# A spectral mixing and feed-forward kernel: batch 0's inverse stage in float32, decode steps, small loads and buffers moved

## The chip, the cores and the metric

The kernel runs on one core of a Trainium2 chip. The metric is the time of one execution in device microseconds (us); lower is better.

## What is computed

```python
def _attn_ref(x, w_r, w_i, b_r, b_i):
    X = np.fft.rfft(x, axis=1)
    Xr, Xi = (X.real.astype(np.float32), X.imag.astype(np.float32))
    Yr = Xr @ w_r - Xi @ w_i + b_r
    Yi = Xr @ w_i + Xi @ w_r + b_i
    lam = 0.01
    Yr = np.sign(Yr) * np.maximum(np.abs(Yr) - lam, 0.0)
    Yi = np.sign(Yi) * np.maximum(np.abs(Yi) - lam, 0.0)
    Y = Yr.astype(np.float64) + 1j * Yi.astype(np.float64)
    y = np.fft.irfft(Y, n=x.shape[1], axis=1)
...
def _moe_ref(x, mu_k, mu_r, w_k, w_v, w_r):
...
    xk = mu_k * x + (1.0 - mu_k) * x_prev
    xr = mu_r * x + (1.0 - mu_r) * x_prev
    k = np.maximum(xk @ w_k, 0.0)
    v = k * k @ w_v
    r = 1.0 / (1.0 + np.exp(-(xr @ w_r)))
    return (r * v).astype(np.float32)
...
def _moe2_ref(x, w_in, w_out):
    h = x @ w_in
    relu6 = np.clip(h + 3.0, 0.0, 6.0)
    g = h * relu6 / 6.0
    return (g @ w_out).astype(np.float32)
```


A Fourier mix along 3072 places, then two feed-forward blocks, for 4 batches of 256 columns. The weights of the second and third part arrive as 64-bit floats. The result has to be close to float32, so most products are made from a high and a low float32r part of each side: three matmuls (high by high, low by high, high by low) for one.

## The kernel before

**Stages.** The transform of 3072 = 96 x 32 places is done as matmuls with tables. For each batch: *s1* (`s1`, 8 steps; a step is two float32 matmuls of 96 rows by 512 columns) goes from x to the scratch `sc_a` in DRAM; *mid* (12 steps) reads `sc_a` and writes `sc_b`; *ib* (8 steps) reads `sc_b` and writes `sc_y`. A middle step j has three parts: `s2` (four float32 matmuls with a table tile `tt`, then `split` into Xh by ScalarE and Xl by VectorE), `mix` (24 float32r matmuls with the weights aw; then yf on VectorE, ym on ScalarE and again yf on VectorE, which is bias and shrinkage; then a split into yh and yl) and `ia` (12 float32r matmuls with the inverse half of a later table tile, an evacuation by ScalarE into iasb, a store). In the loop of `mid` step j issues s2(j), mix(j-1) and ia(j-2).

Behind that come the feed-forward blocks: *units* of a tile of 512 places, `u_r` (pr, one block of twelve 512-column matmuls), four times `u_k` (pk) and `u_v` (acc), into `sc_x`; then the third part (pi, rq, cc, oacc) to the output. A `u_k` makes g = relu, gh = g squared rounded to float32r, g = g squared, gl = g - gh.

**Order.** PE, ScalarE (ACT), VectorE (DVE) and POOL run what the program writes, in the order in which it is written; `stream(first)` is batch 0 up to its first two ib steps, `stream(later)` the rest, one step per unit. So batch 0 runs nearly alone (the *fill*), the others between the units of the batch before them. While batch 0 runs, the weights of the second part are loaded (`stw`) and decoded from the bits of 64-bit floats: `decode` is a generator whose parts (four on VectorE, two on ScalarE, then a split) are advanced by `next(loads)` in the steps listed in `DECODE`. The weights of the third part are decoded the same way (`jobs2`) between the last units, once the stream has ended.

**Queues and buffers.** SyncE (SP) issues nearly all loads and stores, POOL the tables `tt`, f1, fi and tex. A load or store also waits until the one that used its completion counter before it (there are eight, taken in turn) has landed. `load_chunks` keeps `AHEAD` loads of `a` in front of their use, in `AHEAD + 2` buffers. PSUM has two banks in pool `pa` (acc, oacc) and three slots of two banks in `ps`, which s1, s2, mix, ia, ib, pr and pk take in turn; a slot is free when its last reader is done. The tag `ev` gives three buffers for evacuations that are stored: s1sb, iasb, ysb. A tile is written again only when the store from it has landed.

In the trace both s1 and s2 have tiles named s: s1's are on L295, s2's on L332. mix and ia are on the helper's line L164.

## Time and profile before

| | |
|---|---|
| median of 3 runs | 2021.54 us (2019.42 to 2022.19) |
| profiled execution | 2019.82 us, of which 2018.1 are its span |
| busy: TensorE, VectorE, ScalarE, POOL | 98%, 70%, 61%, 2% of the span |
| granted clock of TensorE, mean | 0.99 |
| moved by DMA | 166.26 MB, mean 82 GB/s |

The span runs from the first to the last instruction. Busy time of TensorE is counted from the start of a matmul to its end, and neighbours overlap, so a busy TensorE may still be slow; the granted clock is a share of full speed, 0.50 being 1.2 GHz and 1.00 being 2.4 GHz. "Idle before <- X" names what ended the idle time of an engine. The chain of waits is followed back from the last instruction to what released each step.

### The profile page before, as it was taken

What the parts mean: (1) busy time and instruction counts of PE and PEld (TensorE: products, weight loads), DVE (VectorE), ACT (ScalarE), POOL (GpSimd) and SP (SyncE); (2) the same over time, 40 slices, a digit from 0 to 9 for tenths busy, and PEclk for the clock granted to TensorE, in tenths of its full rate; (3) what the DMA queues carried; (4) which work ended last, traced back from release to release, by engine and by line L of the source; (5) the groups of instructions that cost most, each with busy time, mean ns of one, the idle gap of its engine ahead of it and who ended that gap; (6) DMA issues with size and microseconds to landing.
All of it is one profiled execution on the core that took longest, in us unless ns stands there. A gap on an engine that the chain in (4) does not pass through costs nothing.

```text
span 2018.1 us, 33029 instructions
## 1 busy us (share of the span) xinstructions
PE 1970.9 (98%) x13656; PEld 1812.8 (90%) x13656; DVE 1417.5 (70%) x1721; ACT 1228.0 (61%) x1757; POOL 34.6 (2%) x63
## 2 busy tenths in 40 slices
PE   6789999999999999999999999999999999999998
PEld 4768987988798888777899999999999999999998
DVE  0756654565465658787878877788777887778776
ACT  2556555455445546666557766677667676676665
POOL 0000000000000000000000000000000000000000
PEclk8879999999999999999999999999999999999999
DMA  9675437444643342222101100011001010010100
GB/s 281 198 225 172 118 113 217 150 115 139 210 133 95 107 149 84 76 70 88 42 22 33 32 22 22 25 29 33 22 22 29 25 32 22 22 32 25 30 11 22
DMA packets 106712, 166.26 MB, mean 82 GB/s; under 512 B 12945, under 2 KB 62994, under 8 KB 106562
## 3 DMA queue, kind: packets, MB, share of 16 engines
q1 hardware_dynamic: 96034, 141.76, 22.6%
q0 software_dynamic: 10208, 22.13, 4.5%
q8 instruction: 107, 1.75, 0.4%
q14 instruction: 43, 0.35, 0.1%
q10 hardware_dynamic: 320, 0.26, 0.0%
HBM read 100.81 MB, written 63.31 MB: 81 GB/s over the span
## 4 chain that ended last, share of the span: by engine, by line
PE 81%; DVE 11%; ACT 5%; DMA 2%; issue 1%; ACTq 0%; SPq 0%; DVEq 0%; POOLq 0%
PE oacc L824 25%; PE rq L824 16%; PE acc L164 9%; PE pk L164 8%; PE cc L824 6%; PE mix L164 5%; PE ib L437 3%; PE s L332 3%; PE pr L164 2%; PE s L295 2%; DVE g L574 2%; DVE gl L575 2%; PE ia L164 1%; PE pi L164 1%; ACT gh L573 1%
## 5 line engine op out<-in xcount | busy, mean ns | idle before, releaser
L824 PE MATMUL oacc<-wo_hi,gl 128*128 128x256 f32 x1536 | 425.6, 277 | 1.2 <-DVE gl L765 1.2
L824 PE MATMUL oacc<-wo_hi,gh 128*128 128x256 f32 x1536 | 426.2, 277 | 0.0
L824 PE MATMUL oacc<-wo_lo,gh 128*128 128x256 f32 x1536 | 424.7, 276 | 0.0
L824 PEld LDWEIGHTS oacc<-wo_hi,gl 128*128 128x128 f32 x1536 | 289.2, 188 | 1.8 <-DVE gl L765 1.5
L824 PEld LDWEIGHTS oacc<-wo_hi,gh 128*128 128x128 f32 x1536 | 289.1, 188 | 0.2
L824 PEld LDWEIGHTS oacc<-wo_lo,gh 128*128 128x128 f32 x1536 | 288.5, 188 | 0.0
L756 DVE SCALAR_TENSOR_TENSOR g<-g,c 128x1024 f32<-128x1024 f32 x184 | 225.6, 1226 | 53.5 <-ACT g L752 53.3
L765 DVE TENSOR_TENSOR gl<-g,gh 128x1024 fp32r<-128x1024 f32 x184 | 225.3, 1224 | 50.0 <-ACT gh L762 47.2
L752 ACT ACTIVATE g<-c,half 128x1024 f32<-128x1024 f32 x184 | 212.4, 1154 | 4.9 <-DVE c L747 4.9
L824 PE MATMUL rq<-th,sw 128*128 128x256 f32 x1104 | 212.0, 281 | 0.1
L742 ACT ACTIVATE s<-rq 128x256 f32<-128x256 f32 x184 | 70.7, 384 | 220.1 <-PE rq L824 220.1
L762 ACT ACTIVATE gh<-g 128x1024 fp32r<-128x1024 f32 x184 | 193.9, 1054 | 1.6 <-DVE g L756 1.6
L746 DVE TENSOR_TENSOR c<-rq,s 128x512 f32<-128x512 f32 x184 | 126.8, 689 | 96.5 <-ACT s L742 96.4
L574 DVE TENSOR_TENSOR g<-g 128x1024 f32<-128x1024 f32 x96 | 117.4, 1223 | 106.3 <-ACT gh L573 106.1
L824 PEld LDWEIGHTS rq<-th,sw 128*128 128x128 f32 x1104 | 168.8, 189 | 0.3 <-ACT s L731 0.3
L164 PE MATMUL acc<-gl,wv_hi 128*128 128x512 f32 x384 | 151.2, 394 | 7.3 <-DVE gl L575 7.0
L164 PE MATMUL acc<-gh,wv_hi 128*128 128x512 f32 x384 | 155.6, 405 | 0.0
L824 PE MATMUL rq<-tl,sw 128*128 128x256 f32 x552 | 154.9, 281 | 0.6 <-DVE tl L705 0.6
L164 PE MATMUL pk<-kh,wk_hi 128*128 128x512 f32 x384 | 155.1, 404 | 0.0
L164 PE MATMUL acc<-gh,wv_lo 128*128 128x512 f32 x384 | 149.7, 390 | 0.0
L164 PE MATMUL pk<-kl,wk_hi 128*128 128x512 f32 x384 | 149.6, 390 | 0.0
L164 PE MATMUL pk<-kh,wk_lo 128*128 128x512 f32 x384 | 149.5, 389 | 0.0
(142 smaller groups left out, 4466.6 us busy)
## 6 DMA issues: line engine op xcount, KB each, us to landing
tt<-in_tab_dram POOLq DMA_DIRECT2D x40, 448.0 KB, 4.1
yt<-sc_y SPq DMA_DIRECT2D x23, 608.0 KB, 3.9
a<-in_x_dram SPq DMA_DIRECT2D x64, 192.0 KB, 4.2
sc_a<-s1sb SPq DMA_DIRECT2D x32, 384.0 KB, 4.0
a<-sc_a SPq DMA_DIRECT2D x48, 256.0 KB, 3.7
sc_b<-iasb SPq DMA_DIRECT2D x48, 256.0 KB, 3.9
a<-sc_b SPq DMA_DIRECT2D x64, 192.0 KB, 3.2
sc_y<-ysb SPq DMA_DIRECT2D x32, 384.0 KB, 3.1
```

Of the source, the lines that this page charges most:

```text
L164: nc.tensor.matmul(o, a, c, start=first and i == 0, stop=last and i == n - 1, **kw)
L295: nc.tensor.matmul(p[:N1, 512 * i : 512 * i + 512], f1, flat(a), start=True, stop=True)
L332: mm = lambda c, w, lhs, rhs: nc.tensor.matmul(p[:, c : c + w], lhs, rhs, start=True, stop=True)
L437: nc.tensor.matmul(p[:, q, et, i], lhs, fi, start=True, stop=True)
L574: nc.vector.tensor_mul(g, g, g)
L742: nc.scalar.activation(s[:, 3], q, AF.Copy)
L746: nc.vector.tensor_add(c[:, 1::2], two(rq), s[:, 0:2])
L752: nc.scalar.activation(g, c, AF.Relu, bias=half, scale=1.0 / 6.0)
L756: nc.vector.scalar_tensor_tensor(g, g, 1.0, tmp["c"], op0=ALU.min, op1=ALU.mult)
L762: nc.scalar.activation(h, tmp["g"], AF.Copy)
L765: nc.vector.tensor_sub(hg[i, j][1], tmp["g"], hg[i, j][0].bitcast(F32))
L824: return lambda: nc.tensor.matmul(o, lhs, rhs, start=start, stop=stop, skip_group_check=True)
```

## The change

In batch 0 `ia` is two float32 matmuls with y itself, out of a new table `tab0` (the inverse table whole, not in two parts), into a PSUM bank of `pa`; y isn't split there. Batch 1's s1 steps 0 to 6 all stand behind batch 0's middle; two of them stood ahead of it. f1, tex, the first three table tiles, bias and mu go out on ScalarE's queue; bias is loaded once (64 rows for each of two vectors, not three copies) and spread by VectorE. The mixing weights are loaded at step 3 and split at step 7, ahead of the middle. A decode has six parts instead of five, its run of four VectorE operations being cut in two, and `DECODE` puts them beside the mix steps of the middle (even steps from 12) and into all steps behind it. `AHEAD` is 12 instead of 8, with 6 in places of batch 0. While the third part's weights are decoded, every second u_k squares g on ScalarE instead of VectorE.

```diff
-AHEAD = 8
+AHEAD = 12
...
-FILL = (2, 7)
...
-LOAD_MIX, SPLIT_MIX, LOAD_FI = 7, (9, 10), 20
-DECODE = tuple(range(9, 13)) + tuple(range(13, 39, 2))
+FILL = (0, 7)
...
+VECTORS, LOAD_MIX, SPLIT_MIX, LOAD_FI = 1, 3, 7, 20
+DECODE = tuple(range(9, 12)) + tuple(range(12, 31, 2)) + tuple(range(31, 45))
...
+    tab0 = np.zeros((NP + 2, 128, 2, 320), np.float32)
+    tab0[:NP, :, :, 0:192] = fwd
+    tab0[2:, :, :, 192:320] = inv
...
+        def decode(self, staged, k, q, c, m, lag=1):
+
+            w, new = staged
+            for _ in range(lag - 1):
+                yield
...
+                t = new()
...
                 stt(au, high, 0x80000000, au, op0=ALU.bitwise_and, op1=ALU.bitwise_or)
                 ts(high, high, 0xFFFFF, 0x100000, op0=ALU.bitwise_and, op1=ALU.bitwise_or)
+                yield
                 stt(f, low, 2.0**-32, high, op0=ALU.mult, op1=ALU.add)
                 nc.vector.tensor_mul(f, f, a)
...
-                running.append(w.decode(w.load(stage, *job), *job))
+                running.append(w.decode(w.load(stage, *job), *job, lag=lag))
...
-                    if b == 0:
-                        nc.gpsimd.dma_start(out=tex, in_=ext)
-                        load_t(0, 0)
-                fetch()
+                if b == 0 and s == 4:
+                    nc.scalar.dma_start(out=tex, in_=ext)
+                if b == 0 and s in (4, 6):
+                    load_t(0, s // 2 - 2)
+                fetch(6 if b == 0 and s == 7 else AHEAD)
...
-                t = fp.tile([128, 2, 448], F32R, tag="t", bufs=3, name="tt")
-                c = slice(0 if j < NP else 192, 448 if j >= 2 else 192)
-                nc.gpsimd.dma_start(out=t[:, :, c], in_=tab[j, :, :, c])
+                t = fp.tile([128, 2, 448], F32R if b else F32, tag="t", bufs=3, name="tt")
+                c = slice(0 if j < NP else 192, 192 if j < 2 else 448 if b else 320)
+                eng = nc.gpsimd if b or j > 2 else nc.scalar
+                eng.dma_start(out=t[:, :, c], in_=(tab if b else tab0)[j, :, :, c])
...
-                yy[j] = (y, yh, yl)
+                yy[j] = (y, yh, yl) if b else y
...
-                y, *yy[j] = yy[j]
-                split(y, *yy[j])
+                if b:
+                    y, *yy[j] = yy[j]
+                    split(y, *yy[j])
...
-                yh, yl = yy.pop(j)
+                y = yy.pop(j)
                 t = tt.pop((b, j + 2))[:, :, 192:448]
-                p = ptile("ia")
+                p = ptile("ia") if b else pa.tile([128, 512], F32, tag="acc", name="ia0")
                 for g in range(2):
                     c = slice(256 * g, 256 * g + 256)
+                    if not b:
+                        nc.tensor.matmul(p[:, c], t[:, g, 0:128], y[:, c], start=True, stop=True)
+                        continue
+                    yh, yl = y
...
-                    fetch()
+                    fetch(AHEAD if b or j > 6 else 6)
...
-        nc.gpsimd.dma_start(out=f1, in_=small[:, 0:N1])
+        nc.scalar.dma_start(out=f1, in_=small[:, 0:N1])
...
-                rows = v.partition_broadcast(64).unsqueeze(1).to_broadcast([64, 3, D])
-                nc.sync.dma_start(out=bias[64 * i : 64 * i + 64], in_=rows)
-            nc.sync.dma_start(out=bias[64:65, 0], in_=b_r.partition_broadcast(1))
+                nc.scalar.dma_start(out=bias[64 * i : 64 * i + 64, 1], in_=v.partition_broadcast(64))
+            nc.scalar.dma_start(out=brow[64:65], in_=b_r.partition_broadcast(1))
...
-            nc.vector.tensor_scalar(bias, bias, LAM, None, op0=ALU.subtract)
+            for i in (0, 2, 1):
+                nc.vector.tensor_scalar(bias[:, i], bias[:, 1], LAM, None, op0=ALU.subtract)
+            nc.vector.tensor_scalar(bias[64:65, 0], brow[64:65], LAM, None, op0=ALU.subtract)
...
-                nc.vector.tensor_mul(g, g, g)
+                if jobs2 is not None and j % 2:
+                    nc.scalar.activation(g, g, AF.Square)
+                else:
+                    nc.vector.tensor_mul(g, g, g)
...
-        loads = decoder(wr.jobs + wk.jobs + wv.jobs, stage1)
+        loads = decoder(wr.jobs + wk.jobs + wv.jobs, stage1, lag=2)
...
+            if step == SPLIT_MIX:
+                for w, staged, job in plain:
+                    for _ in w.decode(staged, *job):
+                        pass
+            if step == VECTORS:
                 vectors()
```

How instructions move on an engine shows at three places.

ScalarE's queue at the start of the program, before (s1sb is the evacuation of an s1 step):

```order
L297 ACT_TABLE_LOAD
L297 ACTIVATE s1sb<-s_139 96x1024 [waits PE_49]
L297 ACTIVATE s1sb<-s_149 96x1024 [waits PE_49]
L297 ACTIVATE s1sb<-s_159 96x1024 [waits PE_49]
L297 ACTIVATE s1sb<-s_169 96x1024 [waits DMAHW2_49,PE_49,Activation_49]
```

and with the change:

```order
L496 DMA f_94<-in_small_dram 96x96
L301 ACT_TABLE_LOAD
L301 ACTIVATE s1sb<-s_148 96x1024 [waits PE_49]
L301 ACTIVATE s1sb<-s_158 96x1024 [waits PE_49]
L506 DMA bias<-in_b_r_dram 64x256 [waits DMAHW4_49]
L506 DMA bias<-in_b_i_dram 64x256 [waits DMAHW6_49]
L507 DMA brow<-in_b_r_dram 1x256 [waits DMAHW7_49]
L510 DMA mus<-in_moe_mu_k_dram 128x2x1 [waits DMAHW1_49]
L510 DMA mus<-in_moe_mu_r_dram 128x2x1 [waits DMAHW2_49]
L301 ACTIVATE s1sb<-s_178 96x1024 [waits PE_49]
L301 ACTIVATE s1sb<-s_184 96x1024 [waits DMAHW0_49,PE_49,Activation_49]
L301 ACTIVATE s1sb<-s_194 96x1024 [waits DMAHW5_49,PE_49,Activation_49]
```

Six loads now stand in ScalarE's queue, one ahead of everything and five between the second and the third evacuation, each of the five waiting for the counter of an earlier load of x.

VectorE in two middle steps of batch 0, before (yf and Xl belong to the middle; stt, stw, wr_lo and wk_lo to the decode):

```order
L156 TENSOR_TENSOR yl<-yf,yh 128x512 [waits Activation_49]
L220 TENSOR_TENSOR wr_lo<-stt,wr_hi 128x512
L209 SCALAR_TENSOR_TENSOR stt<-stw,stt 128x512
L210 TENSOR_SCALAR stw<-stw 128x512 [waits DVE_49]
L211 SCALAR_TENSOR_TENSOR stt<-stw 128x512 [waits DVE_49]
L212 TENSOR_TENSOR stt<-stt 128x512 [waits DVE_49]
L204 TENSOR_SCALAR stt<-stw 128x512 [waits DMAHW1_49]
L372 TENSOR_TENSOR yf<-mix,bias 128x512 [waits PE_49]
L377 SCALAR_TENSOR_TENSOR yf<-ym,yf 128x512 [waits Activation_49]
L156 TENSOR_TENSOR Xl<-s_525,Xh 128x768 [waits Activation_49]
```

and with the change:

```order
L160 TENSOR_TENSOR Xl<-s_522,Xh 128x768 [waits Activation_49]
L379 TENSOR_TENSOR yf<-mix,bias 128x512 [waits PE_49]
L226 TENSOR_TENSOR wr_lo<-stt,wr_hi 128x512
L219 SCALAR_TENSOR_TENSOR stt<-stw 128x512 [waits DVE_49]
L220 TENSOR_TENSOR stt<-stt 128x512 [waits DVE_49]
L384 SCALAR_TENSOR_TENSOR yf<-ym,yf 128x512 [waits Activation_49]
L160 TENSOR_TENSOR Xl<-s_577,Xh 128x768 [waits Activation_49]
L379 TENSOR_TENSOR yf<-mix,bias 128x512 [waits PE_49]
L216 SCALAR_TENSOR_TENSOR stt<-stw,stt 128x512
L217 TENSOR_SCALAR stw<-stw 128x512 [waits DVE_49]
```

yl is gone, and the decode's operations, which stood in one run of six ahead of yf in every second step, stand in twos and threes behind each yf.

SyncE's queue in batch 0's first stage, before (a<-in_x are loads of x, sc_a<-s1sb the stores):

```order
L274 DMA a<-in_x_dram 96x512 [waits DMAHW0_49]
L274 DMA a<-in_x_dram 96x512 [waits DMAHW1_49]
L298 DMA sc_a_57<-s1sb 96x1024 [waits DMAHW2_49,Activation_49]
L298 DMA sc_a_57<-s1sb 96x1024 [waits DMAHW3_49,Activation_49]
L274 DMA a<-in_x_dram 96x512 [waits DMAHW4_49,PE_49]
L274 DMA a<-in_x_dram 96x512 [waits DMAHW5_49,PE_49]
L298 DMA sc_a_57<-s1sb 96x1024 [waits DMAHW6_49,Activation_49]
L274 DMA a<-in_x_dram 96x512 [waits DMAHW7_49,PE_49]
L274 DMA a<-in_x_dram 96x512 [waits DMAHW0_49,PE_49]
```

and with the change:

```order
L278 DMA a<-in_x_dram 96x512 [waits DMAHW3_49]
L278 DMA a<-in_x_dram 96x512 [waits DMAHW5_49]
L302 DMA sc_a_57<-s1sb 96x1024 [waits DMAHW0_49,Activation_49]
L278 DMA a<-in_x_dram 96x512 [waits DMAHW3_49]
L278 DMA a<-in_x_dram 96x512 [waits DMAHW4_49]
L302 DMA sc_a_57<-s1sb 96x1024 [waits DMAHW5_49,Activation_49]
L278 DMA a<-in_x_dram 96x512 [waits DMAHW6_49,PE_49]
L278 DMA a<-in_x_dram 96x512 [waits DMAHW7_49,PE_49]
L302 DMA sc_a_57<-s1sb 96x1024 [waits DMAHW0_49,Activation_49]
L302 DMA sc_a_57<-s1sb 96x1024 [waits DMAHW3_49,Activation_49]
```

Twelve loads of x stand ahead of the first store instead of ten; the last four wait for counters that were used in between, three of them by loads on ScalarE's queue (bias twice, brow).

## Rows read from the trace of the kernel before

**Rows 1.** Windows: busy us (instructions) of PE, PEld, DVE, ACT, POOL; clock, DMA share, GB/s
```profile
0.00:50.00 50.00, 34.93 (x120) 20.23 (x120) 3.98 (x11) 14.38 (x15) 4.47 (x11) 0.90 0.95 280
50.00:100.00 50.00, 38.88 (x271) 36.93 (x272) 36.58 (x57) 27.44 (x45) 4.25 (x8) 0.90 0.67 203
...
850.00:900.00 50.00, 47.01 (x203) 37.38 (x202) 41.65 (x54) 30.91 (x39) 0.00 (x0) 1.00 0.28 89
```

**Rows 2.** Chain of waits in order of time, first 400 us: start, us, what
```profile
25.23 4.65 DMA sc_a<-s1sb
30.02 4.08 DMA a<-sc_a
...
122.87 6.24 DMA sc_b<-iasb
129.26 2.60 DMA a<-sc_b
...
148.40 3.62 PE pr L164 x12
...
191.87 2.72 PE pk L164 x12
...
209.64 2.83 PE mix L164 x24
...
215.18 0.71 PE ia L164 x6
215.89 1.30 PE s L332 x8
...
293.96 1.72 PE s L295 x4
...
331.02 1.76 PE ib L437 x16
```

**Rows 3.** Timeline of PE: start, us, what, count, idle before and its end
```profile
5.11 11.29 PE L295 MATMUL s<-a,f 96*96 96x512 f32 x20 [5.11 <-DMA f<-in_small_dram]
...
34.24 0.66 PE L332 MATMUL s<-tt,a 128*128 128x64 f32 x2 [5.67 <-DMA a<-sc_a]
...
54.88 0.80 PE L164 MATMUL ia<-yh,tt 128*128 128x256 f32 x2 [5.80 <-ACT yh L155]
...
71.82 0.39 PE L164 MATMUL mix<-aw_hi,Xh 128*128 128x256 f32 x1 [1.72 <-DVE yf L372]
...
132.00 6.22 PE L437 MATMUL ib<-fi,a 96*128 96x96 f32 x32 [2.98 <-DMA a<-sc_b]
```

**Rows 4.** Windows of 5 us, for the granted clock (third number from the end)
```profile
35.00:40.00 5.00, 5.00 (x20) 5.00 (x20) 0.46 (x2) 1.44 (x2) 0.54 (x1) 0.50 0.56 128
...
140.00:145.00 5.00, 5.00 (x20) 3.92 (x18) 2.20 (x4) 2.35 (x4) 0.00 (x0) 0.50 0.79 247
```

**Rows 5.** VectorE: a group of the first 400 us, a row of its timeline
```profile
L156 DVE TENSOR_TENSOR yl<-yf,yh 128x512 fp32r<-128x512 f32 x26 | 17.8, 684 | 4.3 <-ACT yh L155 4.3
...
68.22 0.68 DVE L209 SCALAR_TENSOR_TENSOR stt<-stw,stt 128x512 uint32<-128x512 uint32 x1
```

**Rows 6.** DMA issues of the first 175 us: count, KB, us to landing
```profile
f<-in_small_dram POOLq DMA_DIRECT2D x1, 36.0 KB, 3.8
...
mus<-in_moe_mu_k_dram SPq DMA_DIRECT2D x1, 1.0 KB, 5.7
```

**Rows 7.** Timeline of SyncE's queue: start, us to issue
```profile
32.65 0.60 SPq L499 DMA_DIRECT2D mus<-in_moe_mu_k_dram  x1
```

**Rows 8.** Groups from 776.6 to 959.1 us: count, busy us, mean ns, idle before
```profile
L164 PE MATMUL acc<-gl,wv_hi 128*128 128x512 f32 x112 | 45.0, 402 | 6.0 <-DVE gl L575 5.7
...
L164 PE MATMUL pr<-kh,wr_hi 128*128 128x512 f32 x28 | 10.9, 389 | 0.0
...
L574 DVE TENSOR_TENSOR g<-g 128x1024 f32<-128x1024 f32 x28 | 34.2, 1222 | 26.6 <-ACT gh L573 26.6
...
L573 ACT ACTIVATE gh<-g 128x1024 fp32r<-128x1024 f32 x28 | 29.4, 1050 | 0.2
```

More of the change, by code (lines that the diff above doesn't have):

```diff
@@ L99, in _tables @@
     tab[2:, :, :, 192:448] = np.concatenate(_pair(inv), 3)
+    tab0 = np.zeros((NP + 2, 128, 2, 320), np.float32)
+    tab0[:NP, :, :, 0:192] = fwd
+    tab0[2:, :, :, 192:320] = inv
     small = np.concatenate([f1, f1.T], 1).astype(np.float32)
-    return [np.ascontiguousarray(a) for a in (tab, ext, small)]
+    return [np.ascontiguousarray(a) for a in (tab, tab0, ext, small)]
 @with_exitstack
@@ L120, in fourier_mix_ffn_kernel @@
     tab: bass.AP,
+    tab0: bass.AP,
     ext: bass.AP,
@@ L190, in load @@
             return w, t
-        def decode(self, staged, k, q, c, m):
-            w, t = staged
-            yield
+        def decode(self, staged, k, q, c, m, lag=1):
+            w, new = staged
+            for _ in range(lag - 1):
+                yield
             hi, lo = self.hi[:, k : k + q, c : c + m], self.lo[:, k : k + q, c : c + m]
@@ L214, in decode @@
                 f = w
-                yield
-                yield
             yield
@@ L220, in decode, with decoder @@
             nc.vector.tensor_sub(lo, f, hi.bitcast(F32))
-    def decoder(jobs, stage):
+    def decoder(jobs, stage, lag=1):
         running = []
-        for n in range(2 * len(jobs) + 5):
-            for r in running:
-                next(r, None)
-            running = running[-3:]
+        for n in range(2 * len(jobs) + lag + 4):
+            running = [r for r in running if next(r, 0) is None]
             if n % 2 == 0 and n // 2 < len(jobs):
                 w, *job = jobs[n // 2]
-                running.append(w.decode(w.load(stage, *job), *job))
+                running.append(w.decode(w.load(stage, *job), *job, lag=lag))
             yield
@@ L284, in take, with fetch @@
             return r
-        def fetch():
-            load_chunks(head["use"] + AHEAD)
+        def fetch(n=AHEAD):
+            load_chunks(head["use"] + n)
         def s1(b, lo, hi):
@@ L862, in fourier_mix_ffn_kernel @@
                 plain = [(w, w.load(stage1, *job[1:]), job[1:]) for w in aw for job in w.jobs]
-                load_t(0, 1)
+            if step == SPLIT_MIX:
[3 more added lines that the diff above has]
+            if step == VECTORS:
                 vectors()
-            if step in SPLIT_MIX:
-                w, staged, job = plain.pop(0)
-                for _ in w.decode(staged, *job):
-                    pass
             if step == LOAD_FI:
@@ L1044 @@
 _INS = ["x", "w_r", "w_i", "b_r", "b_i", "moe_mu_k", "moe_mu_r", "moe_w_k", "moe_w_v", "moe_w_r", "moe2_w_in", "moe2_w_out"]
-_TABLES = ["tab", "ext", "small"]
+_TABLES = ["tab", "tab0", "ext", "small"]
 def kernel(**inputs):
```

15 lines of the change are left out of this document (8 added, 7 removed).

## The prediction

> **What bounds the kernel now.** I read the windows of the whole trace first: from about 180 us on TensorE is busy without a break, except in one later stretch. So only two things can move the end: TensorE's idle or slow time, and TensorE's own work. The chain of waits gives the full-speed price of each piece of work, where pieces stand back to back [rows 2]: a first-stage step s1 1.72 us, a middle step s2 1.30, mix 2.83, ia 0.71, an inverse step ib 1.76, a block of twelve 512-column matmuls (pk, acc, pr) 2.72.
>
> *The fill.* Before the first pr block at 148.40 [rows 2] TensorE does 16 s1 (27.5), 12 middle steps of 1.30 + 2.83 + 0.71 (58.1) and 4 ib (7.0): 92.6 us of work in 148.4. 55.8 us are lost. TensorE's timeline says where [rows 3]: nothing before 5.11 (table f); 5.67 idle before 34.24 (the round trip of sc_a through DRAM); 5.80 before 54.88; 1.72 in every second middle step, as before 71.82; 2.98 before 132.00 (the round trip of sc_b). After the longer gaps the granted clock is 0.50, the 1.2 GHz level, though TensorE is busy: 35 to 40, 140 to 145 [rows 4]. The middle takes 34.24 to 122.87, 7.4 us a step for 4.84 of work, while VectorE is busy 36.6 of 50 us and ScalarE 27.4 [rows 1]: no engine is full, queues that run in order hold each other. At 68.22 VectorE begins four decode operations that stand ahead of yf [rows 5], and mix waits until 71.82 for yf [rows 3], because its PSUM slot is the one yf reads: s2, mix and ia take the three slots in turn.
>
> *The later stretch*, 776.6 to 959.1, where the second weights are decoded: 28 acc, as many pk and 7 pr blocks [rows 8] are 63 x 2.72 = 171.4 us in 182.5. 11.1 us are lost; VectorE waits 26.6 us for gh before its 28 squares of 1.22, TensorE waits for gl [rows 8]; from 850 to 900 VectorE is busy 83%, ScalarE 62% [rows 1].
>
> **The change, part by part.** I walk TensorE through the fill.
>
> *Start and first stage.* f is issued first on ScalarE's queue instead of behind POOL's start. Landing took 3.8 [rows 6], so the first matmul comes at 3.5 to 5.1; I take 4.5. Twelve x loads go out ahead of any store, and two s1 steps of batch 1, with their loads and stores, leave this stage. Against that, five small loads now stand on ScalarE's queue between the second and third evacuation, at 0.60 of issue each if ScalarE's queue is like SyncE's [rows 7]; and the later x loads reuse the completion counters of three of them, so SyncE, with sc_a's second store behind, waits until those have landed. A small load landed after 5.7 [rows 6], in a crowded queue. Each evacuation needs the store three before it to have landed (4.65 [rows 2]), so these delays travel to the eighth. I put the last store's landing at 28.5 (27 to 31) against 25.23 + 4.65 = 29.9, and with 4.08 for the load [rows 2] the middle starts at 32.6 (30 to 35) against 34.24.
>
> Sharing queues: in the first 50 us the DMA engines are 95% busy at 280 GB/s [rows 1], so what shortens this stage is bytes, not queues: four loads of x of batch 1 and two thirds of bias are not moved here. The Trainium skill, "DMA: Bandwidth & Descriptors", section "Issuing engines are not separate DMA queues", says that loads started on another engine run on the same DMA engines and save only issue time. It speaks against this part of the change and the row agrees; by it alone the move to ScalarE's queue would be worth nothing here.
>
> *The middle.* TensorE has been idle for some ten microseconds, so the clock will be at 0.50 as at 35 to 40 [rows 4]: two s2 steps cost twice 2 x 1.30 and the extra pieces of the first, 6.5; mix(0) starts near 39.3, half a microsecond of it slow. The mixing weights are already split, and the first decode waits for a load issued long before, so the 5.80 goes. ia is one float32 product instead of three float32r ones. The nearest row is s2, also float32: 1.30 for four products of 192 columns, 0.325 each, so 0.433 for 256 columns, 0.87 for the two of an ia: +0.16 x 12 = +1.9 us. The Trainium skill, "FP8 and Floating Point Precision", section "TensorE Precision Notes", counts four passes for true float32; three float32r products are three passes, so by it ia would cost 0.71 x 4/3 = 0.95 and the sum 1 us more. A step is then 1.30 + 2.83 + 0.87 = 5.00.
>
> Does TensorE get it? yl (0.684 [rows 5]) leaves VectorE and yh leaves ScalarE in each step; ia has PSUM of its own, so mix takes the slot of the s2 whose split it needs anyway, and yf has a whole step of room; the decode's VectorE work stands in every step with about half, not in every second one with all. VectorE was busy 36.6 of 50 us [rows 1]; even at 7.4 us a step that is 5.4 a step, less 0.68 for yl 4.7 in 5.00, so it has room, if little. I take 5.00 plus 1.5 us of small stalls in all (bounds 0 and 6, half a microsecond a step). mix(0), ten full steps and mix(11): 2.83 + 50.0 + 2.83 = 55.7, so the last mix ends at 39.8 + 55.7 + 1.5 = 97.
>
> *Behind it* come seven s1 and the last two ia, 7 x 1.72 + 2 x 0.87 = 13.8, to 110.8, in place of five s1. They cover the round trip of sc_b: the last ia is done at about 102; its evacuation needs the buffer of the first of these s1, whose store lands near 104.7; then 0.6, a store of 4.65 to 6.24, a load of 2.60 to 4.08 [rows 2]: ib at 113 (111 to 116) against 132.00. A gap of about 2 us is left, and waits for evacuations make another. Before 132.00 a gap of 2.98 was followed by 0.50 until past 145 [rows 3, 4]: 132.00 to 148.40 held 9.0 us of work, 7.4 lost. Here that costs 0 to 7.4; the gap is shorter, I take half, 3.7. Four ib and one s1 (8.8) bring 121.8, the chain to the first kh and kl 0.7, the slow clock 3.7: pr at 126.2 against 148.40, **-22.2**.
>
> *After that*, TensorE had hardly any idle time. Five decode steps leave this place (it costs nothing to lose what was hidden), but the load yt stands behind one more store of sc_y, and a load of sc_a that waits for the last s1's store stands ahead of one: +1 (0 to 3). *More buffers* otherwise cost nothing: look-ahead and buffers grow by four each, so loads wait for the same distance.
>
> *The later stretch.* Half of 28 squares, 14 x 1.22 = 17.1 us, go from VectorE to ScalarE, where a square is 1.05 [rows 8]: 14.7 more. Of 182.5 us that is 9% and 8%: VectorE goes from 83 to 74%, ScalarE from 62 to 70. Where VectorE waited for gh before the square, only 1.22 - 1.05 and a handover are won; where it had a backlog, the full 1.22. The decode's long run of operations is also cut in two. The gain is between nothing (ScalarE's queue becomes the one that holds) and 11.1; I take 7.5, about two thirds, since few of the 28 squares can stay behind a backlog.
>
> Sum: -22.2 + 1 - 7.5 = **-28.7**. The profiled execution took 2019.82 (span 2018.1), the median of the runs is 2021.54, 1.7 above it. So 1991.1 on the one, 1992.8 as a median; I say 1993.
>
> **The rivals.**
>
> *The clock holds and nothing stalls*: no slow ib stretch (-3.7), no stalls in the middle (-1.5), 9.5 instead of 7.5 in the later stretch: 7 us better, **1986**. For it: TensorE is then busy without a gap from 32 to 110. Against: the round trip of sc_b is longer than what is left to hide it.
>
> *The in-order queues hold the middle again*: 5.5 us a step (+4.5) and the whole slow clock at ib (+3.7): **2001**. For it: VectorE's Xl, yf and the last operation of y still form a loop with ScalarE. Against: PSUM no longer ties mix to yf.
>
> *The squares bring nothing*: ScalarE, in order, delays the next g by 1.05, and TensorE's wait for gl stays: +7.5, **2000**. For it: VectorE waits for gh already. Against: both engines are then free for a quarter of the time.
>
> *It doesn't do what it says, and ends slower*: ScalarE's queue holds the first stage. If each of its five small loads kept the next and the evacuations behind it waiting until it had landed, at the slowest landing of the rows, 6.24 [rows 2], and 0.60 to issue [rows 7], that is 34.2 us for a gain of 28.7: **2027**. It decides from 5.7 us each, issue included, which is what mus took to land [rows 6]. Against: the counters they wait for belong to x loads issued in the first microseconds, not to each other.
>
> **How the numbers follow.** Forecast 0.54, clock holds 0.17, middle held 0.13, squares bring nothing 0.11, slower 0.03, everything bad at once 0.02. Around the forecast the bounds are: start of the middle -2.6 to +2.4 (in it the first matmul and the eighth store), stalls -1.5 to +4.5, slow clock -3.7 to +3.7, ib's start -2 to +3, later stretch -3.6 to +7.5. They won't all fall on one side: about 8 down and 10 up, which takes in the two rivals near 2000. Range 1982 to 2004. A difference under 0.2% (4 us) can't be told from no change with this kernel; all cases but the last are beyond it on the fast side. Two bad cases together would still be faster; for all of them at once 0.02 is kept. Faster 0.95, same 0.02, slower 0.03.
>
> **What would show it.** Right: the first s2 at 31 to 34; middle steps 5.0 us apart with no wait of mix for yf; the last mix near 97; the first ib near 113; pr near 126; the stretch of the second decode with under 4 us lost. The clock row of the ib stretch tells 1986 from 1993. Wrong: an s1 evacuation that waits several microseconds for a store held up on SyncE; waits of mix for Xl or yf in the middle; ScalarE waiting nowhere in the later stretch while TensorE waits for gl.

## The result, and the profile after

The changed kernel takes **1998.35 us** (median of 4 runs, 1996.18 to 1999.28) where the kernel before took 2020.9 beside it: a ratio of 0.9887, with a 95% interval of 0.9870 to 0.9904. Its profiled execution took 1999.28 us, with a span of 1997.5. The forecast was 1993 and the range 1982 to 2004: the direction is right, and the time is 5.4 above the forecast.

The span fell by 20.6 us. TensorE's timeline splits that at the first acc block (second weights of the expert stage; before it lies the fill, behind it the rest). It starts at 157.81 instead of 167.18, so the fill gave 9.4. From there to the end it takes 1839.7 instead of 1850.9, so the rest gave 11.2. The forecast had 21.2 and 7.5: more than twice the fill gain that came, and 3.7 too little of the later one. That the time lies in the range is in part luck, since the second error covers a third of the first.

Windows of after, which answer to [rows 1]; columns are busy us and instructions of PE, PEld, DVE, ACT and POOL, then the granted clock, DMA share and GB/s:
```profile
50.00:100.00 50.00, 50.00 (x361) 48.96 (x359) 34.40 (x54) 26.34 (x41) 7.31 (x10) 0.97 0.59 182
850.00:900.00 50.00, 50.00 (x222) 41.42 (x221) 38.58 (x50) 38.11 (x46) 0.00 (x0) 1.00 0.26 88
```
From 50 to 100 TensorE no longer waits (38.88 busy before), and from 850 to 900 neither (222 matmuls instead of 203). So both aims are reached in the steady parts; what is missing lies at the edges of the fill. The chain of waits of after, which answers to [rows 2] (start, us, what):
```profile
19.37 5.88 DMA sc_a<-s1sb
...
25.35 1.03 ACT s1sb L301
...
26.40 3.08 DMA sc_a<-s1sb
...
29.67 5.11 DMA a<-sc_a
...
34.92 4.14 PE s L338 x16
...
41.18 2.99 PE mix L168 x23
44.17 5.25 issue
49.42 2.90 PE s L338 x8
52.32 2.90 PE mix L168 x24
55.22 0.86 PE ia L398 x4
56.08 1.30 PE s L338 x8
57.38 2.74 PE mix L168 x24
```
Two things are to be seen. A middle step is 0.86 + 1.30 + 2.74 = 4.90, without a wait, as forecast (5.00). But after the first mix stands a hole of 5.25 us, marked "issue" since the wait ends with nothing that the chain knows, and the step behind it is slow: s2 2.90 instead of 1.30. The clock's row for that stretch, and one of those at ib, answer to [rows 4]:
```profile
50.00:55.00 5.00, 5.00 (x32) 5.00 (x31) 1.29 (x2) 0.82 (x1) 0.00 (x0) 0.75 0.38 83
...
125.00:130.00 5.00, 5.00 (x19) 3.86 (x19) 3.01 (x5) 2.45 (x6) 0.00 (x0) 0.50 1.02 370
```
What s2(2) waits for is found on ScalarE. Its timeline in after, and the row of the DMA issues of the first 60 us (count, KB, us to landing):
```profile
39.09 0.92 ACT L159 ACTIVATE Xh<-s 128x896 fp32r<-128x896 f32 x1 [11.68 <-PE s L338]
39.09 0.58 ACTq L325 DMA_DIRECT2D tt<-in_tab_dram  x1
```
```profile
tt<-in_tab_dram ACTq DMA_DIRECT2D x1, 320.0 KB, 10.2
```
The third table tile is issued behind the first Xh, at 39.09, and lands 10.2 us later, at 49.3; s2(2) starts at 49.42. In the kernel before, POOL's timeline has the three tiles issued in the first microseconds:
```profile
2.52 1.98 POOL L319 DMA_DIRECT2D tt<-in_tab_dram  x3
```

### The profile page after: what moved, and what is told of

Same layout as the page of the kernel before. It is cut to its first block, busy times and chain, and to the rows that moved or that the text cites. A ratio compares the mean times of both kernels' runs of the same rounds, so it can differ in the third digit from the quotient of the medians.

```text
span 1997.5 us, 32946 instructions
## 1 busy us (share of the span) xinstructions
PE 1961.1 (98%) x13632; PEld 1812.4 (91%) x13632; DVE 1384.1 (69%) x1691; ACT 1241.3 (62%) x1766; POOL 33.8 (2%) x58
## 3 DMA queue, kind: packets, MB, share of 16 engines
q1 hardware_dynamic: 95072, 141.37, 22.6%
## 4 chain that ended last, share of the span: by engine, by line
PE 94%; DVE 3%; ACT 2%; DMA 1%; issue 1%; SPq 0%; ACTq 0%; DVEq 0%
PE oacc L840 25%; PE rq L840 16%; PE acc L168 13%; PE pk L168 12%; PE mix L168 6%; PE cc L840 6%; PE pr L168 3%; PE s L338 3%; PE ib L449 3%; PE s L299 2%; PE pi L168 1%; PE ia L168 1%; PE ia L398 1%; DVE g L772 0%; DMA sc_a<-s1sb 0%
## 5 line engine op out<-in xcount | busy, mean ns | idle before, releaser
L582 ACT ACTIVATE g<-pk 128x1024 f32<-128x1024 f32 x96 | 97.8, 1019 | 88.3 <-PE pk L168 87.9
```

The costliest lines, as they stand in the source:

```text
L582: nc.scalar.activation(g, p, AF.Relu)
```

## The experiments

All are the changed kernel with one edit, unless another base is named. Starts are from TensorE's timeline, in us; "rest" is the span less the start of the first acc block. The ratio is to runs of the kernel before on the same chip.

| kernel | median (lowest to highest) | ratio, 95% interval | first s2 | last mix ends | first ib | first acc | rest |
|---|---|---|---|---|---|---|---|
| before | 2020.9 (2019.42–2022.19) | | 34.24 | 115.20 | 132.00 | 167.18 | 1850.9 |
| after | 1998.35 (1996.18–1999.28) | .9870–.9904 | 34.92 | 102.92 | 121.30 | 157.81 | 1839.7 |
| 1 third tile on POOL | 1992.15 (1990.60–1994.81) | .9843–.9876 | 38.75 | 99.89 | 117.76 | 151.81 | 1839.4 |
| 2 third tile early on ScalarE | 1990.36 (1989.71–1990.96) | .9839–.9868 | 35.89 | 97.02 | 114.38 | 149.49 | 1839.5 |
| 3 run 2 with a fourth buffer | 1993.42 (1990.59–1993.89) | .9852–.9885 | 35.08 | 96.20 | 113.19 | 149.59 | 1839.2 |
| 4 first decode steps later | 1999.88 (1999.00–2000.05) | .9881–.9911 | 35.39 | 103.86 | 121.62 | 158.83 | 1839.3 |
| 5 two s1 ahead of the middle | 1996.74 (1994.06–1998.46) | .9869–.9898 | 35.66 | 101.50 | 118.33 | 154.46 | 1839.3 |
| 6 36 matmuls ahead of ib | 2001.45 (1998.44–2003.55) | .9889–.9918 | 35.36 | 103.33 | 126.95 | 157.05 | 1839.5 |
| 7 12 matmuls ahead of ib | 1995.76 (1994.92–1997.57) | .9867–.9896 | 34.73 | 102.44 | 120.67 | 154.44 | 1839.6 |
| 8 all squares on VectorE | 1997.47 (1996.48–1998.33) | .9870–.9900 | 34.93 | 102.03 | 119.47 | 156.22 | 1839.3 |
| 9 decode uncut | 2007.51 (2006.11–2009.05) | .9922–.9955 | 35.92 | 107.02 | 125.95 | 161.23 | 1844.6 |
| 10 ia in the shared PSUM pool | 1997.57 (1997.25–1997.90) | .9869–.9909 | 35.62 | 104.27 | 121.41 | 156.55 | 1839.5 |
| 11 ia as three products, y split | 1995.75 (1995.45–1996.06) | .9860–.9899 | 35.21 | 99.96 | 118.32 | 154.82 | 1839.5 |
| 12 the edits of 9, 10 and 11 | 2009.68 (2008.57–2009.90) | .9924–.9969 | 35.72 | 106.24 | 126.42 | 162.38 | 1844.4 |

Run 8 has the same code as after up to the first acc block, and reaches it 1.6 us earlier: so far two executions of one fill differ. Runs 6 and 7 share that code up to the first ib; over these four kernels the first s2 lies between 34.73 and 35.36 and the last mix ends between 102.03 and 103.33. The rest differs by 0.5 between kernels whose code is the same there.

### The hole of 5.25: where the third table tile is issued (runs 1 and 2)
```diff
-                eng = nc.gpsimd if b or j > 2 else nc.scalar
+                eng = nc.gpsimd if b or j > 1 else nc.scalar
```


> The kernel after, with the third table tile loaded from POOL's queue again (the first two stay on ScalarE's). Theory: TensorE's idle time from 44.17 to 49.42 in the kernel after is a wait for this tile, whose load stands on ScalarE's in-order queue behind the first Xh and is issued only at 39.09. On POOL nothing stands ahead of it, so the gap of 5.25 goes, and with it the slow stretch behind it (s2 2.90 instead of 1.30): the last mix ends near 96 instead of 102.92, and the time falls by 5 to 8 us, to 1991 to 1993. Rival 1, the DMA engines are the limit there: 320 KB go out while x is loaded, which at 280 GB/s is 1.2 us later for all of the first stage, and TensorE waits at the same place for a load of sc_a instead: 0 to 2 us won. Rival 2, the gap is worth nothing because what follows waits for something else later: the last mix comes earlier, the first pr block does not.

The hole is gone and the time fell by 6.2, within the theory's 5 to 8. But the middle begins 3.8 us later than in after, and the last mix ends at 99.89, not near 96. So the delay of rival 1 is there as well, and more than its 1.2, though its price (0 to 2 us won) is not. The queue of SyncE in this run (start, us to issue):
```profile
11.92 0.32 SPq L302 DMA_DIRECT2D sc_a<-s1sb  x1
13.38 4.18 SPq L278 DMA_DIRECT2D a<-in_x_dram  x2
```
In after the first store went out at 10.31 and the two loads behind it took 1.08 on the queue, from 11.85. So 1.6 us of the delay are there before the first store, and 3 more arise at these loads, with the second store of sc_a behind them. SyncE's waits in the first 20 us of this run name what held the second load (waited for: us in total, times, longest):
```profile
SPq L278 <- DMA bias<-in_b_r_dram: 3.5, 1, 3.5
```
The load of x waited 3.5 us until a bias load from ScalarE's queue had landed, whose completion counter it takes next, as the prediction had it of these loads. In after the two waits for bias are 0.4 and 1.1 us.

So the tile should go out neither among the loads of x nor behind Xh. In run 2 it is issued at the head of the middle, still on ScalarE:
```diff
+                if b == j == 0:
+                    load_t(0, 2)
                 if j < NP:
                     s2(j)
-                load_t(b, j + 2)
+                if b or j:
+                    load_t(b, j + 2)
```


> The kernel after, with the third table tile still on ScalarE's queue, but issued ahead of the first Xh instead of behind it (near 28 instead of 39.09, behind the first stage's work and not beside it as in the run with POOL's queue, where the middle began 3.8 us later). Theory: the middle begins near 35 as in the kernel after, without the gap of 5.25: last mix near 96, first ib near 115, time 1990 to 1992, 6 to 8 us less than the kernel after and 0 to 2 less than with POOL's queue. Rival: the stretch to 40 us is bound by bytes, the tile takes its 1.2 us from the load of sc_a, and the middle begins at 36 to 38; then the time is that of POOL's run, 1992.

ScalarE's timeline of this run, its DMA issues of the first 60 us, and its chain:
```profile
26.65 1.02 ACT L301 ACTIVATE s1sb<-s 96x1024 f32<-96x1024 f32 x1 [2.78 <-DMA sc_a<-s1sb]
26.72 0.55 ACTq L325 DMA_DIRECT2D tt<-in_tab_dram  x1
```
```profile
tt<-in_tab_dram ACTq DMA_DIRECT2D x1, 320.0 KB, 3.8
```
```profile
35.89 6.35 PE s L338 x24
42.24 2.85 PE mix L168 x24
...
94.28 2.74 PE mix L168 x24
```
No hole, no slow step behind it: the middle lasts 61.1 us instead of 68.0, the first acc block comes 8.3 earlier, the time is 8.0 less than after's. This is the theory, with 1 us of the rival at the middle's start (35.89). 1990.36 beats both kernels; the place of one load in a queue was worth 8 us, where the whole change won 22.6.

The Trainium skill, "DMA: Bandwidth & Descriptors", section "Issuing engines are not separate DMA queues", has it that DMAs started by different engines run on the same DMA engines, and that starting them on several engines saves only the time of starting, usually little. Run 1 agrees on the sharing: from POOL's queue the tile still held up x on SyncE's, and TensorE waited 1.36 us for a load of x, until 8.90. What it costs to stand behind other work in a queue is told by the rows of this case alone. The same tile of 320 KB, on the same ScalarE queue, landed at 49.3 behind an activation and at 30.5 ahead of it. Of these 18.8 us, 12.4 are the later issue and 6.4 the longer landing; the DMA engines are at 1.08 from 39 to 44 us in after, but why it took 10.2 to land was not tested.

### What shortens the middle step (runs 9 to 12)

Run 9 takes back the decode's body of the kernel before, for the fill's weights and for the later ones:
```diff
-            for _ in range(lag - 1):
-                yield
+            yield
...
                 ts(high, high, 0xFFFFF, 0x100000, op0=ALU.bitwise_and, op1=ALU.bitwise_or)
-                yield
                 stt(f, low, 2.0**-32, high, op0=ALU.mult, op1=ALU.add)
```


> The kernel after, with the weight decode's body as in the kernel before (four VectorE operations in one row again, all of a block's VectorE work in every second step); the squares stay divided. Theory: the run with all squares on VectorE lost nothing, so the gain of the later stretch is the decode's cut. Then with the cut undone the stretch 750 to 950 loses again. If the divided squares give nothing at all, it is 11 us, and the time is near 2009 to 2010; if either of the two is enough to free the stretch, 0 to 3 us. In the fill, whose decode is the same code, middle steps become up to half a microsecond longer (0 to 6 us more). Rival: the later stretch is free for a third reason; then 222 matmuls in each 50 us stay, and the time moves by under 3 us.

Run 10:
```diff
-                p = ptile("ia") if b else pa.tile([128, 512], F32, tag="acc", name="ia0")
+                p = ptile("ia")
```


> The kernel after, with ia of batch 0 in a slot of the shared PSUM pool again instead of a bank of its own. Theory: s2, mix and ia then take the three slots in turn, mix waits for the slot that yf or the evacuation of ia reads, and a middle step takes 5.5 to 7 us instead of 4.90: the last mix comes 6 to 20 us later. Rival: with the split of y gone and the decode cut, VectorE and ScalarE are early enough and the slot is free in time: 4.9 to 5.1, no change.

Run 11 gives batch 0 the path of the later batches (yh, yl, the split inverse table, all table loads on POOL), with the bank kept:
```diff
-                    if not b:
+                    if False:
                         nc.tensor.matmul(p[:, c], t[:, g, 0:128], y[:, c], start=True, stop=True)
                         continue
```


> The kernel after, with ia of batch 0 as three float32r products of a split y again (in the bank of its own, decode cut); the tables then come as float32r, all on POOL's queue, so it is compared with the run that has the third tile on POOL's queue, whose middle steps took 4.90. Theory 1, VectorE and ScalarE have room: ia falls to 0.71, yl adds 0.68 to VectorE and yh 0.6 to ScalarE, and a step takes 4.75 to 4.9: the float32 product was not needed for the middle's speed. Theory 2, the two extra operations of a step stand ahead of yf or Xl on their in-order queues: 5.5 to 7.4, the last mix 7 to 30 us later than 99.9.

The steady steps, from the chains: after 4.90; run 10 also 4.90 (the rival); run 9 5.47 (10.94 for two); run 11 5.28 (10.55 for two), between its two theories. In run 9's chain, ym of every second step:
```profile
66.47 0.72 ACT ym L382
...
77.41 0.72 ACT ym L382
```
Between the two this chain stands on ScalarE and VectorE alone and never reaches TensorE. Run 11 is 2.6 us faster than after, but that is the hole, which it hasn't, with its tables on POOL's queue. Against run 1, whose third tile is on that queue too, it is 3.6 slower, and its middle takes 64.8 instead of 61.1. The chain of run 11 shows what a pair of steps hangs on:
```profile
66.88 2.84 PE mix L168 x24
...
69.74 0.70 DVE yf L379
70.47 0.72 ACT ym L382
71.19 0.62 ACT stt L213
...
72.46 0.58 ACT iasb L403
73.04 0.71 ACT Xh L159
73.78 0.96 DVE Xl L160
74.73 0.61 DVE yl L160
...
75.39 0.74 PE ia L168 x4
76.12 1.30 PE s L338 x8
```
The path leaves TensorE after mix, goes over yf, the decode's two activations, the evacuation of ia, Xh, Xl and yl, and comes back at ia: two in-order queues, gone through once in a pair of steps, in which TensorE has work for less time than that. Without yh and yl, ia needs only y, which in after is ready 2.0 to 2.5 us before it. That is why the float32 ia pays although its 0.86 is longer than three float32r products (0.74 here, 0.71 in [rows 2]). Such an ia is six float32r matmuls in the code and in [rows 2] (x6), not the twelve that the section on the kernel before gives it. The Trainium skill, "FP8 and Floating Point Precision", section "TensorE Precision Notes", counts four passes for float32; from 0.71 for three products, ia would by that be 0.95, an estimate, if a pass costs what a float32r product costs. The trace has 0.86, a ratio of 1.21 to 0.71 and not 1.33. The count itself isn't contradicted: two matmuls of four passes in 0.86 are 0.108 a pass, six products in 0.71 are 0.118 each.

In run 12 the three edits stand together:

> The kernel after, with three parts undone at once: ia of batch 0 as three float32r products of a split y (tables on POOL's queue), in a slot of the shared PSUM pool, and the decode uncut. Alone, undone, they made a middle step 5.28, 4.90 and 5.47 us against 4.90. Theory 1, they only cost together, since VectorE's and ScalarE's queues run out of room when both kinds of work are there: a step takes 6.8 to 7.4, as in the kernel before, and the last mix ends 20 us or more behind 99.9. Theory 2, they add up: 4.90 + 0.38 + 0 + 0.57 = 5.85; then what is missing to 7.4 belongs to the place of the decode steps (every s2 step instead of every mix step), the one part of the middle not undone here. In both the later stretch is that of the run with the uncut decode, about 5 us longer than after.

```profile
60.91 0.72 ACT ym L382
...
73.06 0.72 ACT ym L382
```
ym of every second step comes 12.15 us after the last, so a step takes 6.07. The sum of the single losses gives 5.85; together they cost a little more, 6.07. And that is all: in the chain of the kernel before, the same two steps take 12.12 (s2 at 63.97, 76.10, 88.22). The expectation's 7.4, from the prediction, was no step at all: it was the stretch from 34.24 to 122.87 divided by twelve, with the hole of 5.80, its slow stretch and the tail behind the last mix in it. The three parts together bring back the whole step; what the place of the decode steps might add is not needed for it.

### The later stretch (runs 8 and 9)
```diff
-                if jobs2 is not None and j % 2:
+                if False:
```


> The kernel after, with every second square of the later stretch back on VectorE. Theory: of the gain, about 11 us is this one line; windows of 50 us from 750 to 950 hold 203 to 215 matmuls again instead of 222, TensorE waits for gl again, and the time rises by 9 to 12 us, to about 2009. Rival: the stretch became free of waits because the decode's long run of VectorE operations is cut in two; then undoing the squares costs 0 to 4 us.

No difference: windows of this run, and below them of run 9 (cut undone, squares divided):
```profile
900.00:950.00 50.00, 50.00 (x222) 41.37 (x222) 43.75 (x55) 34.30 (x42) 0.00 (x0) 1.00 0.24 78
```
```profile
900.00:950.00 50.00, 47.97 (x204) 39.20 (x204) 35.28 (x45) 35.67 (x43) 0.00 (x0) 0.97 0.23 74
```
What TensorE waits for in run 9 is gl again (a group from 740 to 960; the last numbers are idle time and what ended it):
```profile
L168 PE MATMUL acc<-gl,wv_hi 128*128 128x512 f32 x140 | 55.3, 395 | 3.0 <-DVE gl L591 3.0
```
With all squares on VectorE that engine is busy 88% of a window, and TensorE does not wait; with half of them on ScalarE but the decode uncut, VectorE is busy 71%, and TensorE waits. Busy share was the wrong thing to read. The four cases of "rest" give the prices: neither part 1850.9 (the kernel before), squares alone 1844.6 and 1844.4, cut alone 1839.3, both 1839.7. The cut takes all 11. Where the decode is uncut, 6 us lie between the kernel before and the runs with the squares divided; the kernel before lacks the other edits too (in the decode, when the tile stt is taken), so that these 6 are the squares' is likely but not shown. Where it is cut, dividing them gives nothing. Run 9's span is 8.3 longer than after's: 4.9 here, between its theory's two figures, and 3.4 in the fill.

### The slow clock ahead of pr (runs 6 and 7)
```diff
                 n0 = N1 + 4 * c * N1
+                if (b, c) == (0, CHUNKS[0]):
+                    p = ptile("warm")
+                    w = aw[0].hi
+                    for _ in range(36):
+                        nc.tensor.matmul(p[:, 0:512], w[:, 0, 0:128], w.rearrange("p k n -> p (k n)"), start=True, stop=True)
```


> The kernel after, with 36 float32r matmuls of 512 columns, whose result nobody reads, put on TensorE ahead of the first ib, into its idle time from 112.39 to 121.30. Theory: the slow clock from 120 to 142 comes from that idle time. At 0.227 each the added matmuls take 8.2 us, the clock stays at 1.00, and the four ib, the s1 and the first pr, 21.37 us from 121.30 to 142.67, come down towards their full-speed 3.52 + 1.72 + 3.52 + 2.72 = 11.5; loads of sc_b that land late will keep some of it: the time falls by 5 to 10 us. Rival 1: the clock is low there for another reason (a slow stretch of its own, or the load on other engines): granted 0.50 as before, no gain, or a loss of up to 1 us where an added matmul stands in the way. Rival 2: the clock stays up, but ib then waits for its loads: the gain is under 3 us.

> The kernel after, with 12 instead of 36 matmuls, whose result nobody reads, ahead of the first ib: in the run with 36 the first of them began at 118.64, so 12 x 0.227 = 2.7 us end at 121.4, where the kernel after began its first ib. Theory 1, the slow clock does cost, and 36 were too many (ib began at 127.11 instead of 121.30): granted clock 1.00 again, and the first pr block ends 4 to 8 us before 142.67, the time falls by as much. Theory 2, the loads of sc_b and the chain from the second ib over xf, kh and kl set the end of this stretch, and TensorE's clock does not: TensorE waits as much as it is faster, the first pk block comes within 1.5 us of 144.43, the time within 2 us of the kernel after.

In after TensorE waits ahead of ib in two places, and then runs at half clock; two rows of its timeline, and the windows behind the one shown above:
```profile
115.38 3.67 PE L299 MATMUL s<-a,f 96*96 96x512 f32 x8 [2.14 <-ACT s1sb L301]
121.30 1.99 PE L449 MATMUL ib<-fi,a 96*128 96x96 f32 x8 [2.25 <-DMA a<-sc_b]
```
```profile
130.00:135.00 5.00, 5.00 (x20) 3.91 (x18) 2.82 (x5) 3.07 (x5) 0.00 (x0) 0.50 1.04 350
135.00:140.00 5.00, 5.00 (x21) 4.71 (x21) 2.65 (x7) 3.01 (x7) 0.00 (x0) 0.50 0.76 241
```
This stretch in run 7:
```profile
120.00:125.00 5.00, 5.00 (x38) 4.43 (x37) 1.47 (x3) 2.35 (x4) 0.00 (x0) 1.00 1.01 356
125.00:130.00 5.00, 4.59 (x32) 3.48 (x31) 3.73 (x8) 2.93 (x7) 0.00 (x0) 1.00 0.93 310
130.00:135.00 5.00, 2.86 (x13) 2.00 (x12) 2.10 (x4) 2.13 (x3) 0.00 (x0) 0.93 1.02 350
```
With matmuls in the second wait, the clock stays at 1.00 from 120 to 130, where after falls to 0.50. So the wait ahead of ib brings it down; the one ahead of the s1 steps, 1.36 us in run 7, doesn't do it alone. The other runs agree: where ib follows with at most 0.37 us of wait (runs 1, 9 and 12) the window behind its start has 1.00, and in the seven others, with 1.73 to 6.51, the clock is at 0.50 for 10 us or more.

In after the slow clock makes 21.37 us (121.30 to 142.67) of 11.5 us of work: 9.9 lost on TensorE. In run 7 the first pr block starts 6.1 earlier (132.18), but the first acc block only 3.4, and only 1.8 against run 8, whose code is that of after up to there; the median is 2.6 below after's. From the last mix to the first acc block run 7 takes 52.0 us, after 54.9 and run 8 54.2, but run 10, with the slow clock as well, 52.3. So at most 3.4 of the 9.9 reach that block, and how much exactly these runs can't tell. In between, from 130 to 135, TensorE is busy 2.86 of 5: by run 7's chain, ysb, the evacuation of ib, waits for a store of sc_a that takes 4.77 us while the DMA engines are at 1.02, and xf, kh and kl come behind it. So both theories hold in part: the clock costs, and what follows the second ib sets most of the end. Run 6 had 24 matmuls too many: ib began 5.7 us later, and instead of falling by its theory's 5 to 10 us the median rose by 3.1.

### What holds the edges (runs 3, 4 and 5)
```diff
-                    sb = fp.tile([128, 4, D], F32, tag="ev", bufs=3, name="iasb")
+                    sb = fp.tile([128, 4, D], F32, tag="ev", bufs=4, name="iasb")
```
(the same for s1sb and ysb; base is run 2)

> The kernel with the third table tile issued early (1990.36), and four buffers instead of three in the ring that s1sb, iasb and ysb share. Theory, the ring holds the stretch ahead of the first ib: in the kernel after the last ia ended at 108.08, but its evacuation began at 112.46, because the buffer was still being stored by a first-stage step, and the first stage's eighth evacuation (25.35) waited 5.88 for a store. With four buffers the eighth evacuation comes 1 to 3 us earlier, the last iasb 2 to 3 us after its ia, the first ib 2 to 4 us before 114.38: 1983 to 1988. Rival, bytes bind both stretches (DMA share 0.9 to 1.0): stores and loads only wait in another place, each takes longer to land, and the time is within 2 us of 1990.

The rival. The eighth evacuation came 3.8 us earlier than in run 2 (22.88 against 26.65), but the stores of the stage were no faster for it; the chain of run 3:
```profile
22.88 1.02 ACT s1sb L301
...
25.09 6.33 DMA sc_a<-s1sb
```
The last store took 6.33 and landed at 31.4; in run 2 it was issued 2.6 later, took 4.33 and landed at 32.0. Ahead of ib the theory's ring was there: the last iasb began 0.4 us behind its ia (101.76), not 4.4 as in after. But the load of sc_b behind its store (issued at 102.38) went out only at 109.79, when that store had landed, 7 us later instead of 2.9 in after. SyncE's waits from 100 to 125:
```profile
SPq L278 <- DMA sc_b<-iasb: 2.8, 1, 2.8
```
The first ib came 1.2 us earlier than in run 2, and the slow clock took that back: 17.0 us from ib to pr instead of 14.8. The first acc block came at 149.59 against 149.49. The median is 3.1 above run 2's, which even the rival's 2 us don't cover; no gain is shown.

Run 4 puts the first three decode steps, with their loads of 512 KB, three steps later:
```diff
-DECODE = tuple(range(9, 12)) + tuple(range(12, 31, 2)) + tuple(range(31, 45))
+DECODE = tuple(range(12, 15)) + tuple(range(16, 31, 2)) + tuple(range(31, 46))
```


> The kernel after, with the first three steps of the weight decode (each the load of a block of weights, and work on VectorE) put three steps later, behind the first two middle steps. Theory: the load of sc_a that starts the middle took 5.11 us instead of 4.08, because two loads of weights of 512 KB stand ahead of it on SyncE (26.75 and 27.64); without them it lands in about 4.1 and the middle starts near 33.9 instead of 34.92. The time moves by 0 to 2 us only. Rival: the DMA engines are full with x and the tables anyway, the load takes over 5 us again, and the middle starts at 34.9.

The rival again: the load of sc_a took 4.85 and the middle began at 35.39. The median rose by 1.5 us.

Run 5 (the numbers of the steps are moved by two with it):
```diff
-FILL = (0, 7)
+FILL = (2, 7)
```


> The kernel after, with two first-stage steps of batch 1 ahead of the middle again, as in the kernel before, and five behind it. Theory, the stretch to 50 us and the one from 105 to 145 are both bound by bytes (DMA share 0.9 to 1.1 in nearly every 5 us): four loads of 192 KB and two stores of 384 KB, 1.5 MB at 280 to 320 GB/s, 5 us, go from the later stretch to the earlier. The middle begins at 38 to 40 instead of 34.92, and the first acc block, 157.81, moves by -2 to +3 us only, the time within 3 us of the kernel after. Rival 1, the two steps fill TensorE's idle time ahead of the middle (15 to 35) for nothing: the middle still begins near 35 and everything behind is 3 to 5 us earlier. Rival 2, with five steps instead of seven behind the middle the round trip of sc_b is less covered, and the time is 3 to 6 us longer.

The middle began at 35.66, not at 38 to 40, so the theory's first half falls: the two steps cost the first stage 0.7 us, as rival 1 says. The first acc block came 3.4 earlier than after's, as far as rival 1 had it, but 2.4 of that is a shorter hole (2.83 instead of 5.25: the tile landed after 7.9 instead of 10.2). What is left, 1 us, is less than the 1.6 by which two executions of one fill differ. Where those two s1 steps stand makes no difference that these runs can tell.

## Why the prediction was right and wrong

**Right: the mechanism in the middle.** PSUM, split and decode were read as queues that hold each other, and a step of 5.00 without waits was forecast; it is 4.90. Of the three reasons given, the decode's cut is worth 0.57 a step when it alone is undone, the split of y 0.38, and the bank of its own nothing. The size of the loss was read wrongly as 7.4 a step: it was 6.06, and the rest were the hole, its slow stretch and the tail behind the last mix.

**Wrong: "so the 5.80 goes".** That hole did go. In the chain of the kernel before it is a load of decode weights, for which VectorE waits ahead of yf:
```profile
41.63 8.79 DMA stw<-in_moe_w_r_dram
...
50.79 0.70 DVE yf L372
```
In after yf begins at 44.19, behind the first mix at once. But another hole opened, because the step looked at what the middle had waited for, the mixing weights and this load, and not at every load that the edit moved. The third table tile changed its queue from POOL, where it was issued with the first two from 2.52 on, to ScalarE behind Xh. Its 5.25, and 1.8 of slow clock behind it, are twice the 3.6 by which the middle is longer than forecast (68.0 instead of 64.4); without them the middle was 3.4 shorter than walked, for the 1.5 of stalls that didn't come, the 0.10 a step, and a start 0.9 quicker. Run 2 has no such hole: last mix at 97.02 (forecast 97), first ib at 114.38 (113). That the first agrees so well is luck: its middle begins 3.3 later than forecast and is as much shorter.

**Wrong in size: the start of the middle**, 34.92 instead of 32.6. The last store landed at 29.5 and not 28.5, and the load of sc_a took 5.11 and not 4.08. The early f did help: the second evacuation came at 9.85 (11.28 in the kernel before). But then ScalarE's queue issues the five small loads; its timeline of after:
```profile
9.86 0.54 ACTq L506 DMA_DIRECT2D bias<-in_b_r_dram  x1
...
12.91 1.93 ACT L301 ACTIVATE s1sb<-s 96x1024 f32<-96x1024 f32 x2 [2.04 <-DMA bias<-in_b_r_dram]
```
They take 3.0 us, at 0.6 each as walked, and the third evacuation is back at 12.91 (13.00 in the kernel before). SyncE's loads of x wait 1.5 us for two of them to land, as the prediction said they would. From 17 us on, the last four evacuations each wait for a store to land, and run 3 shows a store that was asked for 2.6 us earlier landing only 0.6 earlier. But bytes are not the whole of it: from 10 to 15 us the DMA engines are at 0.77 (1.11 in the kernel before). Two s1 steps less in the stage did not show (run 5).

**Wrong in size: the first ib and the clock.** ib came 18.4 behind the last mix, not 16; the last iasb began at 112.46, 9.5 behind the last mix and not 7.7, because the store of sc_a ahead of it in its buffer, issued at 106.70, landed at 112.35 and not near 104.7. Two gaps of about 2 us were forecast and are there, but they cost the whole slow stretch, not half: 17.0 from ib to pr instead of 13.2. Half was a choice between nothing and all, without a row for it. The four parts, 2.3 at the start, 3.6 in the middle, 2.4 at ib and 3.8 in the clock, make up the 12.1 by which pr came late (138.3 instead of 126.2). At pr the slow clock does cost that much (run 7 gains 6.1 there); at the first acc block it is worth 3.4 at most.

**Right in sign, wrong in cause: the later stretch.** 7.5 was put on the squares, with the cut decode as a side remark. The cut alone gives 11, the squares on top of it nothing. "The squares bring nothing" was a rival and came true, but not at its price: it had TensorE's wait for gl stay. The wrong step is the balance of busy shares (83 to 74%); what mattered is how the decode's six VectorE operations fall: in one step all six (the run of four, the last of the block ahead and the first of the next) and none in the other, against three and three. Run 9 changes this and loses 4.9 with the squares divided. That they delay gl because they stand ahead of it in VectorE's order is read from the program and from TensorE's wait for gl, not tried by itself.

**Open:** the small loads on ScalarE, the early load and split of the mixing weights and the larger look-ahead were not undone alone. That the small loads cost the first stage what the early f had won is read from the one trace; the middle's start was not tried without them.

## What to carry to other kernels

When an edit moves a load to another engine, look up what stands ahead of it in that engine's order and when that runs: the same 320 KB landed 19 us earlier one place ahead of an activation. Where an in-order engine serves a pipeline, cut a side job into equal pieces per step before work is moved between engines; its busy share says little. And before a stretch is shortened by earlier requests or more buffers, see whether the DMA engines are full there: here the transfers then only took longer.

## What the runs showed of the hardware

A low clock held through full activity: TensorE was busy 5.00 of 5.00 us in each window from 125 to 140 with the granted clock at 0.50, after two waits of 2.14 and 2.25 us; 3.0 us of matmuls in the second wait kept it at 1.00 until 130. And a slow TensorE cost the kernel far less than it lost itself, at most 3.4 of 9.9 us at the first acc block, since a faster one waited for transfers instead.

A load waited for another engine's: in run 1 a load of x on SyncE stood 3.5 us until a bias load from ScalarE's queue had landed, whose completion counter it takes next.
